# A new order for the beginning of an attention, gated-MLP and soft-MoE kernel: first scores, turned probabilities, and weight blocks in pairs

## The chip, the cores and the metric

The kernel runs on one core of one Trainium2 chip. The metric is the device time of one execution in microseconds (us). Three executions of the kernel before took 1693.24, 1691.48 and 1683.35 us, median 1691.48 us.

## The reference

Three stages follow each other, all in float32:

```python
# attention, 8 batches x 12 heads, 448 positions, head size 64
q_n, k_n = rmsnorm(q, g_q), rmsnorm(k, g_k)
attn = softmax(q_n @ k_n.T / 8)          # rows sum to 1 (+1e-9)
x = (attn @ v) as (3584 tokens, 768)
# gated MLP, 768 -> 1536 -> 768
x = (sigmoid(x @ w_gate) * (x @ w_val)) @ w_out
# soft MoE: 32 slots, 8 experts of 4 slots, 768 -> 1024 -> 768
logits = x @ phi
d = softmax(logits over tokens); c = softmax(logits over slots)
out = c @ expert_mlps(d.T @ x)
```

## The kernel before

**Tiling.** The heads are taken in 48 pairs, six pairs to a batch. For one pair (`slot`) the kernel loads q, k and v, normalises q and k (`prep_a` to `prep_g`), and makes seven score tiles of up to 128 rows by 448. The gated MLP of a batch (the "products", `mm`, line 805) starts when all six pairs of that batch are done. It has 72 units over the twelve weight blocks of `w_gate` and `w_val` and 36 units over `w_out`. The soft MoE follows the MLP batch by batch, and the experts come at the end.

**One score tile in the first twelve pairs** (batches 0 and 1, done in float32) goes through five steps. `score`: TensorE makes the tile `sc` (L434, L428 for the tail). `soft_max`: VectorE scales it and takes the row maximum (L470). `soft_exp`: ScalarE makes `p` or `ps` with row sums (L490). `soft_hi`: TensorE turns the probabilities in four transposes (`pq`, L499). `soft_lo`: ScalarE copies the turned tile out of PSUM into a buffer (L532). When all tiles of a pair are there, `weigh` makes the row sums (`rs`, L576 and L582) and the product with v (`av`, L590) on TensorE, and three small operations (L609 to L612) put the result into `ck`, from which the MLP reads. From pair 12 on the attention runs in float16 along another path, which the change does not touch.

**Weights.** The float32 weights go through a conversion into two float16 halves before the MLP of batch 0 can use them. A gate/value block has two tiles (gate and value, 128 x 768 each). One tile costs a load into one of two `wr` buffers (L712), three VectorE operations that move bits (`to_f32`: L694, L697, L700) into a scratch region `x` of the still unused `gt` buffer (a ring of `NX` regions), and one ScalarE pass that finds a size (`amax`, L677). For a block, two small TensorE products spread the sizes over the partitions (`am`, L129), five or six small VectorE operations make scales (`w_scale`), and then each tile takes two ScalarE scalings (L742, L743) and one GpSimd subtraction (L744). `w_out` has twelve more tiles with the same bit moves and `amax`, two scalings (L772, L773), one subtraction (L774) and a store to a DRAM scratch `wos`, from which the MLP's second half loads `wo`.

**What sets the order.** All work is entered in an agenda, a table of numbered steps: `at(g, fn)` puts a function at step g. A head pair takes 18 steps (`G0` holds the starts), the MLP of batch 0 starts at step `M0` = 115, and each batch of it takes 108 steps with six products in a step. The list `LEN` sets the steps of pairs 6 to 11. The constants at the top (`KN`) place the conversions: before, blocks 0 to 5 sit at steps 18, 33, 48, 63, 78 and 93, blocks 6 to 11 at 111, 114, ... 126, and the `w_out` tiles every fourth step from 117. Up to step 259 the agenda gives only a first order: the tile layer (`schedule_with_timeline_sim=True` on the launch line) reorders each engine's queue within the dependences by a timeline that it computes. From step 259 on the order of the agenda holds as it is (`manual_schedule`).

Within an engine instructions run in the order of its queue. TensorE's scores, transposes, `am` products and MLP products share one queue. VectorE's row maxima share one with the bit moves, ScalarE's exponentials with `amax`, the scalings, the copies and the MLP's sigmoid. In the trace each change between exponentials (L490) and sigmoids (L811) shows an ACT_TABLE_LOAD.

Of the kernel before, what the change touches and what calls it, by code (L numbers as in the profile page):

```python
# [23 lines left out]
def kernel(  # L24
# [26 lines left out]
    NP = H // 2  # L51
# [87 lines left out]
    pe_t = wte[:, 3072 * 7:3072 * 12]  # L139
# [89 lines left out]
    def v_first():  # L229
        x = gt.rearrange("p f a s -> p (f a s)").bitcast(F32)[:, 0:6 * S]  # L230
        sp.dma_start(out=x, in_=v[0].rearrange("h s d -> (h s d)").rearrange("(p e) -> p e", p=128))
        t = smp.tile([128, 8], F32, tag="vam", name="vam")
        vec.tensor_reduce(out=t[:, 6:7], in_=x, axis=AX.X, op=ALU.max, apply_absolute_value=True)
        vec.tensor_scalar(out=t[:, 6:7], in0=t[:, 6:7], scalar1=1e-30, scalar2=None, op0=ALU.max)
# [381 lines left out]
    def slot(j):  # L616
# [7 lines left out]
        for i, o in enumerate((0, 0, 5, 5, 10, 10, 14) if j < JP else (0, 2, 5, 7, 10, 13, 15)):  # L624
# [5 lines left out]
                (3, lambda i=i: soft_hi(j, i)),  # L630
                (4, lambda i=i: soft_lo(j, i)),
# [811 lines left out]
```

## Time and profile before

| | |
|---|---|
| the profiled execution's own time | 1691.47 us |
| its span in the trace | 1689.7 us |
| instructions | 26467 |
| TensorE busy | 1562.3 us (92%) |
| VectorE busy | 1055.4 us (62%) |
| ScalarE busy | 936.6 us (55%) |
| GpSimd busy | 634.7 us (38%) |
| first score product starts | 30.12 us |
| first MLP product starts (end of "stage 1" below) | 168.17 us |
| last product with v of pair 11 ends (end of "stage 2") | 413.3 us |

A row of a timeline gives the start, the busy time, the engine, the line, the operation, what it writes and reads, the shape and the count, and in brackets how long its engine had been idle and who ended that. A row of a windows view gives for a stretch the busy time and number of instructions of each engine, then the TensorE clock that was granted (1.00 is full), the share of DMA time and GB/s. A row of a groups view gives busy time and the mean in ns of one, then the idle time of the engine just before the group's instructions and what ended it. On TensorE each float32 product appears as two records.

### The profile page before, as it was taken

The numbers are of one execution on the slowest core, as the hardware profiler recorded it, in microseconds if no ns is written. First come the engines' busy times: TensorE is split into PE (matmuls) and PEld (weight loads), VectorE is DVE, ScalarE is ACT, GpSimd is POOL, SyncE is SP. The second block draws the span as 40 slices with busy tenths as digits, with TensorE's granted clock in tenths as the row PEclk, the third lists the DMA queues.
The fourth block names the chain that finished last, engine by engine and source line by source line (L and its number), as shares of the span: only waits on it lengthen the run. The fifth ranks groups of instructions, "written<-read, shape, count | busy, mean of one in ns | idle before, by whom it ended". The sixth has DMA issues, their size and how long they took to land.

```text
span 1689.7 us, 26467 instructions
## 1 busy us (share of the span) xinstructions
PE 1562.3 (92%) x9065; PEld 777.8 (46%) x9065; DVE 1055.4 (62%) x2602; ACT 936.6 (55%) x1795; POOL 634.7 (38%) x725
## 2 busy tenths in 40 slices
PE   3887678999999999999999999999999999999985
PEld 1444334454454454545444545454545454555323
DVE  6677876545667777767776777677767663310214
ACT  3777668744766566656655665466656663211113
POOL 3445533336234535454545454535454530000000
PEclk9898789999999999999999999999999999999876
DMA  6344455325448755774688468756884566444899
GB/s 204 91 132 147 148 164 161 103 71 127 92 109 175 178 106 138 179 185 95 148 163 189 92 153 164 159 108 138 180 183 96 129 141 191 149 153 150 315 376 328
DMA packets 508021, 266.55 MB, mean 158 GB/s; under 512 B 403568, under 2 KB 476016, under 8 KB 507760
## 3 DMA queue, kind: packets, MB, share of 16 engines
q1 hardware_dynamic: 500976, 227.13, 53.6%
q10 hardware_dynamic: 6912, 37.75, 7.2%
q8 instruction: 71, 1.16, 0.3%
q14 instruction: 62, 0.51, 0.1%
HBM read 162.96 MB, written 15.73 MB: 106 GB/s over the span
## 4 chain that ended last, share of the span: by engine, by line
PE 48%; DVE 8%; ACT 8%; DMA 5%; issue 3%; SPq 2%; POOL 0%; ACTq 0%; POOLq 0%; DVEq 0%
PE mm L805 32%; DMA uni<-pst 4%; PE av L597 4%; PE sc L451 3%; DVE pst L548 2%; ACT pst L509 2%; PE so L961 2%; PE hp L1180 1%; PE tx L948 1%; ACT p L490 1%; DVE sc L470 1%; PE po L1232 1%; ACT sgf L811 1%; DVE ss L272 1%; ACT L490 1%
## 5 line engine op out<-in xcount | busy, mean ns | idle before, releaser
L805 PE MATMUL mm<-ck,wt 128*128 128x448 f16 x3456 | 706.1, 354 | 0.9 <-DVE ck L612 0.9
L805 PEld LDWEIGHTS <-wt 128*128 128x128 f16 x3456 | 330.7, 98 | 323.9 <-issue 40.2
L805 PE MATMUL mm<-gt,wo 128*128 128x448 f16 x1728 | 347.5, 353 | 2.5 <-DMA wo<-wos 2.4
L509 ACT ACTIVATE pst<-p,sm 128x448 f16<-128x448 f32 x252 | 168.2, 668 | 222.5 <-DVE sm L505 133.6
L548 DVE SCALAR_TENSOR_TENSOR pst<-p,sm,pst 128x448 f16<-128x448 f32 x252 | 204.6, 812 | 96.3 <-ACT pst L509 87.5
L511 POOL COPY pst<-pst 128x64 f16<-128x64 f16 x252 | 63.9, 254 | 516.7 <-ACT pst L509 516.7
L490 ACT ACTIVATE p<-sc,sm 128x448 f32<-128x448 f32 x286 | 179.6, 628 | 126.5 <-DVE sc L470 123.5
L805 PEld LDWEIGHTS <-wo 128*128 128x128 f16 x1728 | 166.4, 98 | 165.0 <-issue 12.6
L470 DVE TENSOR_SCALAR_CACHE_REDUCE sc<-sc,scal 128x448 f32<-128x448 f32 x252 | 171.5, 681 | 15.8 <-PE sc L451 9.3
L305 POOL TENSOR_TENSOR rr<-ss,nhalf 128x16 f32<-128x16 f32 x48 | 149.1, 3107 | 48.2 <-DVE ss L275 27.6
L451 PE MATMUL sc<-qkt 128*128 128x448 f16 x432 | 116.9, 353 | 0.2 <-DMA qkt<-uni 0.2
L502 DVE TENSOR_SCALAR sm<-sm 128x1 f32<-128x1 f32 x252 | 37.3, 148 | 100.8 <-ACT p L490 100.3
L597 PE MATMUL av<-uni 128*64 128x448 f16 (+1 forms) x792 | 89.8, 361 | 6.7 <-DMA uni<-pst 6.7
L821 DVE TENSOR_TENSOR gt<-sgf,gt 128x448 f16<-128x448 f32 x96 | 76.3, 795 | 11.2 <-ACT gt L820 11.1
L820 ACT CAST gt<-sgf 128x448 f16<-128x448 f32 x96 | 53.5, 557 | 52.4 <-DVE sgf L816 48.6
L816 DVE SCALAR_TENSOR_TENSOR sgf<-mm,fcomp,sgf 128x448 f32<-128x448 f32 x84 | 56.9, 678 | 38.6 <-PE mm L805 38.3
L811 ACT ACTIVATE sgf<-mm,kgate 128x448 f32<-128x448 f32 x96 | 58.3, 632 | 39.7 <-PE mm L805 39.1
L470 DVE TENSOR_SCALAR_CACHE_REDUCE sc<-sc,ss 128x448 f32<-128x448 f32 x84 | 56.2, 684 | 28.5 <-PE sc L434 24.6
L265 POOL TENSOR_TENSOR qn<-rq 128x512 f32<-128x512 f32 x47 | 59.4, 1264 | 33.6 <-DMA rq<-in_q_dram 28.8
L597 PEld LDWEIGHTS <-uni 128*64 128x64 f16 (+1 forms) x792 | 43.5, 110 | 56.3 <-issue 29.9
L811 ACT ACT_TABLE_LOAD x51 | 65.4, 1283 | 4.3 <-PE mm L805 3.4
L265 POOL TENSOR_TENSOR kn<-rk 128x512 f32<-128x512 f32 x47 | 54.7, 1164 | 30.2 <-PE qt L385 17.5
(230 smaller groups left out, 2092.6 us busy)
## 6 DMA issues: line engine op xcount, KB each, us to landing
wo<-wos ACTq DMA_DIRECT2D x48, 768.0 KB, 4.8
wt<-in_moe_w_dram SPq DMA_DIRECT2D x18, 1024.0 KB, 9.7
x<-in_moe_w_dram SPq DMA_DIRECT2D x12, 1024.0 KB, 10.7
vl<-in_v_dram SPq DMA_DIRECT2D x42, 224.0 KB, 2.7
rq<-in_q_dram SPq DMA_DIRECT2D x48, 192.0 KB, 2.7
rk<-in_k_dram SPq DMA_DIRECT2D x48, 192.0 KB, 2.8
wr<-in_moe_w_gate_dram SPq DMA_DIRECT2D x12, 768.0 KB, 4.4
wr<-in_moe_w_val_dram SPq DMA_DIRECT2D x12, 768.0 KB, 4.4
```

Of the source, the lines that this page charges most:

```text
L265: pool.tensor_tensor(out=x, in0=raw[j][i], in1=raw[j][i], op=ALU.mult)
L305: pool.tensor_tensor(out=rr, in0=ss, in1=nhalf, op=ALU.pow)
L451: pe.matmul(out=ps, lhsT=qk[:, 3 * h, 128 * t + 128:128 * t + 256], rhs=qk[:, 3 * h + 1 + n, TAIL:512], start=(n == 0), stop=(n == 1),)
L470: vec.tensor_scalar(out=ps, in0=ps, scalar1=ne, scalar2=3e38, op0=ALU.mult, op1=ALU.min, accum_out=sm[:, 1:2])
L490: act.activation(out=p, in_=ps, func=AF.Exp, scale=-1.0 if KN.get("ACC", 0) else esc, bias=sm[:, 1:2], accum_out=total)
L509: act.activation(out=st[:, 0:S], in_=p, func=AF.Copy, scale=sm[:, 3:4])
L511: pool.tensor_copy(out=st[:, S:S + TAIL], in_=st[:, 0:TAIL])
L548: ins = vec.scalar_tensor_tensor(out=st[:, S + TAIL:], in0=p, scalar=sm[:, 3:4], in1=st[:, 0:S], op0=ALU.mult, op1=ALU.subtract)
L597: pe.matmul(out=ps[64 * h:64 * h + 64, :], lhsT=vs[0:kk, hl, h, tv, :], rhs=pt[h][0:kk, tp, :], start=(n == 0), stop=(n == len(passes) - 1),)
L805: pe.matmul(out=ps, lhsT=l, rhs=r, start=(n == 0 and m == 0), stop=(n == last and m == len(terms) - 1))
L811: act.activation(out=sgm, in_=mm_t.pop(("g", f)), func=AF.Sigmoid, scale=kgate[:, b % 2, f:f + 1])
L821: later(2, lambda: vec.tensor_tensor(out=gt[:, f, 1, :], in0=gf, in1=gt[:, f, 0, :], op=ALU.subtract))
```

## The change

The change has four parts, three of them by constants.

1. **The beginning.** The gains are loaded from ScalarE's queue before everything else (`gains_load`), together with a dummy exponential that loads the table. The search for the largest v of batch 0 (`v_first_max`, then `am` and its scale) leaves the beginning and stands at steps 4, 6 and 8. The copies that make `sel` move to step M0+20, and `phi` goes straight to its place, with three copies at M0+30 instead of four at the start.
2. **The turn of P.** For pairs 0 to 11 `soft_hi` and `soft_lo` stand six and seven steps behind their scores instead of three and four. The next scores of a pair stand five steps behind.
3. **Weights in twos.** Blocks 2n and 2n+1 share one `am` of four columns and one set of scales. Blocks 0/1 are entered at step 2, then 28, 54, 80, 104 and 122 (`GV`), the second block's tiles six steps later (`GD`), the scalings at 16 and 17 steps (`GW`). So eight of twelve blocks are entered within batch 0's attention instead of six. The scratch ring has six regions instead of four, and the turned P of pairs 0 to 5 goes to the buffer `uni` instead of to the part of `wt` that blocks 7 to 11 will fill.
4. **Room.** Pairs 6 to 11 take 18 steps each instead of 28 and five times 16, and the `w_out` tiles start ten steps later (`WOF` 12 instead of 2).

```diff
-KN=json.loads('{... "WOF": 2, ... "NX": 4, ... "LEN": [28, 16, 16, 16, 16, 16], ...
-  "ORD": "sel qk0 a0 g qk1 w b0 c0 d0 e0 f0 g0 a1 v0 vf v1 phi", ...}')
+KN=json.loads('{... "WOF": 12, ... "NX": 6, ... "LEN": [18, 18, 18, 18, 18, 18], ...
+  "ORD": "gl qk0 sel a0 qk1 w b0 g c0 d0 e0 f0 g0 a1 v0 vf v1 phi", ...
+  "VF": 4, "GV": [2, 28, 54, 80, 104, 122], "GW": 16, "GD": 6}')
-    pe_t = wte[:, 3072 * 7:3072 * 12]
...
+    def v_first_max():
         t = smp.tile([128, 8], F32, tag="vam", name="vam")
-        vec.tensor_reduce(out=t[:, 6:7], in_=x, axis=AX.X, op=ALU.max, apply_absolute_value=True)
+        vec.tensor_reduce(out=t[:, 6:7], in_=vam_t.pop("x"), axis=AX.X, op=ALU.max, apply_absolute_value=True)
         vec.tensor_scalar(out=t[:, 6:7], in0=t[:, 6:7], scalar1=1e-30, scalar2=None, op0=ALU.max)
         vam_t[0] = t
-        vamax_spread(0)
-        vamax_scale(0)
...
-                        pt = (pe_t if j < NP else uni)[:, 3584 * n:3584 * n + 3584]
+                        pt = uni[:, 3584 * n:3584 * n + 3584]
...
-                (3, lambda i=i: soft_hi(j, i)),
-                (4, lambda i=i: soft_lo(j, i)),
+                (3 + 3 * (j < JP), lambda i=i: soft_hi(j, i)),
+                (4 + 3 * (j < JP), lambda i=i: soft_lo(j, i)),
...
+    def w_spread(f):
+        w_t["m", f] = spread_max(w_t["s", f // 2][:, 0:4], 4)
...
+        def gains_load():
+            gl = first["gl"] = p1.tile([128, 2, D], F32, tag="t3", name="gl", bufs=3)
+            for i, g in enumerate((g_q, g_k)):
+                act.dma_start(out=gl[:, i, :], in_=g.unsqueeze(0).to_broadcast([128, D]))
+            act.activation(out=scal[:, 2:3], in_=nhalf1, func=AF.Exp)
...
+        at(KN["VF"], v_first_max)
+        at(KN["VF"] + 2, lambda: vamax_spread(0))
+        at(KN["VF"] + 4, lambda: vamax_scale(0))
+        at(M0 + 20, blocks_of_sel)
+        at(M0 + 30, more_columns)
...
+            for n in range(2):
+                for i in range(2):
+                    if f + n >= EW:
+                        at(g + KN["GD"] * n, lambda n=n, i=i: w_load(f + n, i))
+                    at(g + 2 + KN["GD"] * n + i, lambda n=n, i=i: w_bits(f + n, i))
+            e = g + KN["GW"]
+            at(e - 2, lambda: w_spread(f))
+            at(e - 1, lambda: w_scale(f))
+            at(e - 1, lambda: gate_scales(0, f, f + 2))
+            for n in range(2):
+                at(e + n, lambda n=n: w_split(f + n))
```

What the tile layer makes of it is seen in the engines' queues. Lines of the changed kernel are one lower in the middle of the file and up to twelve higher at its end (L434 is now L433, L805 now L808). Three places follow.

TensorE, the first rows of its queue, before (`gt`, `qt`: gains, q and k turned; `vam`: the largest v):

```order
L1292 MATMUL gt<-ident,gl 128x128
L388 MATMUL qt<-ident,rq 64x128 x8
L385 MATMUL qt<-ident,kn 128x128 x4
L129 MATMUL am<-ident,vam 128x128
L434 MATMUL sc<-qkt 128x448 x4
L499 MATMUL pq<-ident,p 128x128 x4
```

and now:

```order
L1301 MATMUL gt<-ident,gl 128x128
L387 MATMUL qt<-ident,rq 64x128 x8
L384 MATMUL qt<-ident,kn 128x128 x4
L433 MATMUL sc<-qkt 128x448 x4
L498 MATMUL pq<-ident,p 128x128 x8
L498 MATMUL pq<-ident,ps 128x128 x4
L129 MATMUL am<-ident,vam 128x128
```

The `am` product of v stood ahead of the first four scores and stands behind them and three turned tiles.

VectorE, the queue ahead of pair 0's first row maxima, before (`gt<-wr`: bit moves of a weight tile; `ss`: sums of squares):

```order
L233 TENSOR_REDUCE vam<-gt 128x1
L1303 COPY gt<-pl 128x6x32 x4
L234 TENSOR_SCALAR vam<-vam 128x1
L694 TENSOR_SCALAR gt<-wr 128x768
L133 TENSOR_REDUCE vam<-am 128x1
L697 SCALAR_TENSOR_TENSOR gt<-wr,gt 128x768
L121 TENSOR_SCALAR sg<-vam 128x1
L272 TENSOR_REDUCE ss<-qn 128x8
L700 SCALAR_TENSOR_TENSOR gt<-wr,gt 128x768
L225 RECIPROCAL sg<-sg 128x1
L470 TENSOR_SCALAR sc,sm<-sc,ss 128x448 x2
```

and now:

```order
L699 SCALAR_TENSOR_TENSOR gt<-wr,gt 128x768
L693 TENSOR_SCALAR gt<-wr 128x768
L274 TENSOR_SCALAR ss<-ss 128x16
L469 TENSOR_SCALAR sc,sm<-sc,ss 128x448
L696 SCALAR_TENSOR_TENSOR gt<-wr,gt 128x768
...
L234 TENSOR_REDUCE vam<-gt 128x1
L308 TENSOR_SCALAR ss<-rr,scal 128x8
L469 TENSOR_SCALAR sc,sm<-sc,ss 128x448
L1313 COPY gt<-gt 128x6x32 x3
```

Before, three weight tiles and the search in v stood ahead of the first maximum. Now one tile and the start of the next do, and three maxima stand ahead of the search in v. Up to the first maximum of pair 1 there are now five tiles and two thirds of a sixth in the queue, and there were four. The sixteen `sel` copies stand in VectorE's second row before and now.

TensorE early in the MLP of batch 0, before, where single `am` products stand:

```order
L805 MATMUL mm<-ck,wt 128x448
L129 MATMUL am<-ident,wa 128x128
L434 MATMUL sc<-qkt 128x448 x2
L499 MATMUL pq<-ident,p 128x128 x4
L499 MATMUL pq<-ident,ps 128x128 x4
```

and now, at the first `am` behind the MLP's start:

```order
L808 MATMUL mm<-ck,wt 128x448
L129 MATMUL am<-ident,wa 128x128 x4
L433 MATMUL sc<-qkt 128x448 x2
...
L498 MATMUL pq<-ident,ps 128x128 x4
L498 MATMUL pq<-ident,p 128x128 x4
```

Before, single `am` products of fresh tiles stood between products, the scores and their own turned tiles with nothing between (44 products without any score had gone ahead). Now four `am` stand together, nine products stand where "..." is, and the turned tiles behind them belong to earlier scores. Behind the product with v of pair 11 the queues of all engines are the same but for names.

More of the change, by code (lines that the diff above doesn't have):

```diff
@@ L1275 @@
         EW = KN.get("EW", 1)
+        first = {}
+        def gains_load():
[3 more added lines that the diff above has]
+            act.activation(out=scal[:, 2:3], in_=nhalf1, func=AF.Exp)
         def gains():
-            gl = p1.tile([128, 2, D], F32, tag="t3", name="gl", bufs=3)
-            for i, g in enumerate((g_q, g_k)):
-                sp.dma_start(out=gl[:, i, :], in_=g.unsqueeze(0).to_broadcast([128, D]))
+            gl = first["gl"]
             gm = smp.tile([128, 4], F32, tag="wa", name="gm")
@@ L1299, in slots_to_columns, with more_columns @@
         def slots_to_columns():
-            pl = p1.tile([128, KD, NS], F32, tag="t3", name="pl", bufs=3)
-            sp.dma_start(out=pl, in_=phi.rearrange("(c p) s -> p c s", p=128))
-            for m in range(4):
-                vec.tensor_copy(out=phr[:, :, m, :], in_=pl)
+            sp.dma_start(out=phr[:, :, 0, :], in_=phi.rearrange("(c p) s -> p c s", p=128))
+        def more_columns():
+            for m in range(1, 4):
+                vec.tensor_copy(out=phr[:, :, m, :], in_=phr[:, :, 0, :])
         def w_first():
@@ L1316 @@
         ops = dict(
-            sel=make_sel, qk0=lambda: load_qk(0), g=gains, qk1=lambda: load_qk(1), w=w_first,
+            sel=make_sel, gl=gains_load, qk0=lambda: load_qk(0), g=gains, qk1=lambda: load_qk(1), w=w_first,
             a0=lambda: prep_a(0), b0=lambda: prep_b(0), c0=lambda: prep_c(0), d0=lambda: prep_d(0),
@@ L1324 @@
         assert not ops
[L1326 to L1336 removed]
+        at(KN["VF"], v_first_max)
[3 more added lines that the diff above has]
+        at(M0 + 30, more_columns)
+        def gv(g, f):
+            assert g + KN["GW"] <= M0 + 12 * (f // 2), "gv late"
+            for n in range(2):
[9 more added lines that the diff above has]
+                at(e + n, lambda n=n: w_split(f + n))
         def wo(g, f):
@@ L1341, in wo @@
             at(g + KN.get("WB", 2), lambda: wo_split(f))
-        NPRE = KN.get("NPRE",4)
-        for f in range(NPRE):
-            gv(G0[NP] - KN.get("PS",20) * (NPRE - f), f)
-        for f in range(NPRE, KF):
-            gv(M0 + KN.get("GO",0)+KN.get("GS",6) * (f - NPRE), f)
+        for n, g in enumerate(KN["GV"]):
+            gv(g, 2 * n)
         for f in range(KF):
```

40 lines of the change are left out of this document (16 added, 24 removed).

## The prediction

> **What bounds the kernel now.** I read the busy times by stretch first, with the cuts at the first score, the first MLP product, the end of the weight conversions and the end of pair 11's product with v.
>
> ```profile
> core 0: us, PE busy (x) PEld busy (x) DVE busy (x) ACT busy (x) POOL busy (x), PEclk, DMA share, GB/s
> 0.00:30.12 30.12, 4.16 (x23) 2.97 (x23) 17.49 (x49) 5.74 (x10) 12.92 (x16) 1.00 0.77 232
> 30.12:168.16 138.04, 116.39 (x623) 59.16 (x622) 100.47 (x237) 100.95 (x220) 63.53 (x50) 0.89 0.42 124
> 168.16:345.00 176.84, 142.34 (x790) 73.52 (x790) 124.06 (x261) 129.57 (x220) 69.60 (x49) 0.90 0.49 140
> 345.00:413.30 68.30, 67.16 (x406) 34.17 (x405) 31.19 (x75) 31.06 (x70) 28.52 (x27) 1.00 0.36 102
> 413.30:1689.70 1276.40, 1232.23 (x7230) 607.98 (x7228) 782.21 (x1981) 669.26 (x1276) 460.12 (x584) 0.98 0.66 165
> 140.00:160.00 20.00, 14.73 (x84) 7.80 (x82) 19.12 (x34) 13.75 (x30) 11.60 (x7) 0.88 0.54 160
> 240.00:320.00 80.00, 69.37 (x398) 34.56 (x398) 50.72 (x117) 65.60 (x112) 32.64 (x24) 0.98 0.49 127
> ```
>
> From 345 us on TensorE is the bound (67.16 of 68.30, then 1232 of 1276 us). Before that no engine is: in the second and third row VectorE and ScalarE are both busy 70 to 73% of the time, and TensorE waits 22 and 34 us and runs at a clock of 0.89 and 0.90. The order behind 413.3 us is the same in both kernels, so I take these 1276.4 us as unchanged, and the question is when pair 11 ends. What TensorE waits for, first between 30 and 168 us, then between 168 and 413 us:
>
> ```profile
> PE pq L499 <- ACT ps L490: 11.5, 9, 2.7
> PE pq L499 <- ACT p L490: 7.8, 7, 2.2
> ```
>
> ```profile
> PE am L129 <- ACT wt L677: 18.6, 3, 10.8
> PE pq L499 <- ACT p L490: 6.8, 4, 3.7
> PE qt L385 <- ACT uni L532: 3.5, 2, 2.6
> ```
>
> In the first stretch it is the turn of a tile that waits for that tile's exponential. In the second it is `am`, which waits for the size of a weight tile and holds up the whole queue. These are the two waits at which the change is aimed.
>
> **The beginning.** The timeline of TensorE, then single rows of the other engines:
>
> ```profile
> 12.58 0.45 PE L1292 MATMUL gt<-ident,gl 128*128 128x128 f32 x1 [12.58 <-DVE gl L1290]
> 15.86 1.09 PE L385 MATMUL qt<-ident,kn 128*128 128x128 f32 x4 [0.92 <-ACT qkt L396]
> 29.40 0.79 PE L129 MATMUL am<-ident,vam 128*128 128x128 f32 x2 [12.45 <-DVE vam L234]
> ```
>
> ```profile
> 10.77 0.23 DVE L1282 TENSOR_TENSOR ggn<-gl 128x64 f32<-128x64 f32 x1 [3.16 <-DMA gl<-in_g_k_dram]
> 11.16 2.92 POOL L305 TENSOR_TENSOR rr<-ss,nhalf 128x16 f32<-128x16 f32 x1 [9.86 <-DVE ss L275]
> 16.98 0.59 ACT L400 COPY qkt<-qt 128x512 f32<-128x512 f32 x1 [1.25 <-PE qt L385]
> 25.53 2.94 DVE L233 TENSOR_REDUCE vam<-gt 128x1 f32<-128x2688 f32 x1
> 47.44 0.69 DVE L470 TENSOR_SCALAR_CACHE_REDUCE sc<-sc,ss 128x448 f32<-128x448 f32 x1 [0.24 <-PE sc L434]
> ```
>
> Two waits go. VectorE stood 3.16 us for the gains, and the scale of pair 0's rows (L275, then GpSimd's L305) stood behind. With the gains issued first I take about 2.8 us off. Pair 0's q and k are turned at 16.98 + 0.59 = 17.57 us, yet TensorE then idles to 29.40 us for the `am` of v. With `am` behind the scores they start at 17.57 - 2.8, about 15 us, instead of 30.12.
>
> Of these 15 us little reaches the end of pair 0, since VectorE's queue now brings weight tiles there. From the first maximum (about 19 us, behind one tile) to that of pair 1 its rows add up to 22.6 us: seven maxima at 0.61 start to start, 2.94 for v, nearly five tiles at about 2.45, and small ones. Two `wr` buffers, each reloaded behind the last bit move of its tile, add about 2 us. So pair 1 starts at about 44 us, where the row above has 47.44: 3.5 us of time and 1.7 tiles (4 us) of work ahead. The dummy exponential, the fourth `phi` copy and the `sel` copies (which the queue leaves where they were) I set at nothing; together they are under 2 us of engines that wait there anyway.
>
> **Stage 1, to the first MLP product.** The groups of 0 to 168 us, VectorE's and ScalarE's:
>
> ```profile
> L470 DVE TENSOR_SCALAR_CACHE_REDUCE sc<-sc,ss 128x448 f32<-128x448 f32 x45 | 30.3, 682 | 8.5 <-PE sc L434 6.6 <-PE sc L428 1.9
> L697 DVE SCALAR_TENSOR_TENSOR gt<-wr,gt 128x768 int32<-128x768 int32 x16 | 18.6, 1160 | 0.0
> L700 DVE SCALAR_TENSOR_TENSOR gt<-wr,gt 128x768 int32<-128x768 int32 x16 | 15.7, 980 | 0.0
> L694 DVE TENSOR_SCALAR gt<-wr 128x768 int32<-128x768 int32 x16 | 13.3, 831 | 4.7 <-POOL wt L744 4.7
> ```
>
> ```profile
> L677 ACT ACTIVATE wt<-gt 128x768 f16<-128x768 f32 x16 | 13.5, 845 | 16.8 <-DVE gt L700 16.1 <-DVE su L536 0.3
> L743 ACT ACTIVATE gt<-gt,wa 128x768 f32<-128x768 f32 x14 | 12.6, 932 | 0.0
> L742 ACT ACTIVATE wt<-gt,wa 128x768 f16<-128x768 f32 x14 | 12.3, 932 | 2.4 <-DVE wa L735 2.4
> ```
>
> The new queue has 20 tiles' bit moves ahead of the end of stage 1 and 16 tiles' scalings, for 16 and 14. VectorE's work there rises from 118.0 us (17.49 + 100.47) by 4 x (0.83 + 1.16 + 0.98) = 11.9 us and falls by about 3 for the scales made in twos: 127 us. ScalarE's rises from 106.7 by 4 x 1.03 + 4 x 0.93 = 7.8 to 114.5 us. So this stage does more work and gains only if the engines fill. They should: a turn now stands behind the next scores, so TensorE has 0.5 to 4 us of other work while an exponential is made, and the 19.3 us of the first wait view shrink. I bound the filling by the table: 73% as now, 95.6% as in 140 to 160 us (19.12 of 20). From 15 us on VectorE has 127 - 8 = 119 us left. At 73% the stage ends at 178 us, at 95% at 140. I take 85%, the middle: 155 us, 13 us earlier than 168.16.
>
> One thing speaks against more. ScalarE now gets up to eight scalings in a row (8 x 0.93 = 7.5 us) ahead of a `ck` and a copy of turned tiles, and was given four before. While they run TensorE has a product with v and one to three scores, about 4 to 5 us.
>
> The clock could add to the gain. An `am` among products takes 0.38 us, one behind a long wait 0.80:
>
> ```profile
> 182.83 0.38 PE L129 MATMUL am<-ident,wa 128*128 128x128 f32 x2
> 196.17 0.80 PE L129 MATMUL am<-ident,wa 128*128 128x128 f32 x2 [10.84 <-ACT wt L677]
> ```
>
> The Trainium skill ("TensorE: Matmul & The Clock Gate", Part 1) says that the clock falls to half behind about 3.4 us of idleness and comes back behind as much work; these rows agree. By it a TensorE without long waits would need some 14 us less for the 142.34. I leave this out of the sum, as ScalarE and not TensorE sets the pace below.
>
> **Stage 2, to pair 11's product with v.** The single `am` products are gone from TensorE's queue, pairs 6 to 11 are spread evenly, and a tile's turn has a dozen products ahead of it. So the 18.6 us wait should vanish. What is late next is ScalarE. It has 129.57 + 31.06 = 160.6 us here, less the 7.8 us moved to stage 1, so 152.8. Behind the last `w_out` tile of the new queue stand some 28 us of it, so the dense part has 125 us. The rows that are dear in it:
>
> ```profile
> L490 ACT ACT_TABLE_LOAD x10 | 12.8, 1283 | 0.2
> L772 ACT ACTIVATE hl<-x,wa 128x768 f16<-128x768 f32 x12 | 11.2, 930 | 5.9 <-DVE wa L771 5.9
> L677 ACT ACTIVATE hl<-x 128x768 f16<-128x768 f32 x12 | 10.1, 845 | 10.5 <-POOL hl L774 5.0 <-DVE wa L734 3.9 <-DVE x L700 1.7
> ```
>
> At 73% these 125 us take 171, at 90% 139. I take the 82% of 240 to 320 us (65.60 of 80.00), the densest stretch where both kinds of work ran: 152 us. TensorE's own work there is about 118 us at full clock, so it waits for ScalarE. Behind it come 237 products and the attention of two pairs. A product takes (403.84 - 399.30) / 24 = 0.189 us:
>
> ```profile
> 399.30 4.70 PE L805 MATMUL mm<-gt,wo 128*128 128x448 f16 x24
> 403.84 0.60 PE L499 MATMUL pq<-ident,ps 128*128 128x128 f32 x4
> ```
>
> That is 45 us, and about 31 us for the attention, as in the 68.30 us now. Stage 2 takes 152 + 76 = 228 us, for 245.1 before: 17 us less.
>
> A table load costs the dense part 1.28 us each, twenty times:
>
> ```profile
> 201.09 1.28 ACT L490 ACT_TABLE_LOAD   x1
> 202.38 0.63 ACT L490 ACTIVATE p<-sc,sm 128x448 f32<-128x448 f32 x1
> ```
>
> The Trainium skill ("ScalarE: Activation LUTs", What ACT_TABLE_LOAD costs) gives 1283 ns for a load, as here, and 1380 ns more for draining the engine, 2.66 us a switch. By that 20 switches would cost 53 us instead of 26. No run shows the drain: the work ahead ends at 201.08, the exponential starts 1.29 us later. The row decides.
>
> **Sum.** 155 + 228 = 383 us for 413.3, so 30.3 us less. The profiled span becomes 1659.4 us; with the 1.8 us between span (1689.7) and time (1691.47, the median of the runs to 0.01 us) it is 1661 us.
>
> **Rivals.** *The engines fill.* With 93% of VectorE in stage 1 (15 + 128 = 143 us) and 90% of ScalarE in stage 2 (139 + 76 = 215) pair 11 ends at 358: 1636 us. For it: 140 to 160 us shows 95.6%. Against it: both queues are in order, and each waits for the other (16.1 us of `amax` for L700).
>
> *Filling stays at 73%.* 178 + 171 + 76 = 425 us: 1703 us. The beginning is then swallowed by the work moved ahead. For it: VectorE's and ScalarE's shares are the same 70 to 73% in two stages with different orders; the ring of six regions still makes the third tile of each group of four wait for GpSimd's subtraction of the group before. Against it: the 19.3 and 18.6 us of waits by name.
>
> *The runs of eight scalings go uncovered.* Six pairs of blocks, each holding up the copies and `ck`, and so TensorE, by 7.5 us: 45 us against the 8 us won by pair 1, 1728 us; with TensorE's 4 us in between half is covered, 1707. It makes the kernel slower by over 1% from 4.2 us uncovered a run. Against it: the runs of four cost TensorE no named wait.
>
> **How the numbers follow.** I give my sum (1645 to 1674) 62%, the filling engines 17%, unchanged filling (1675 to 1708) 16%, the uncovered runs 5%. So faster by over 1% has 0.79, within 1% 0.16, slower 0.05; 1% is about what a measurement of this kernel tells from no change. The range of 8 in 10 is 1638 to 1686: down to the filled engines, up into unchanged filling.
>
> **What would show it.** Right: the first scores at 14 to 16 us, the first maximum at 18 to 21 and that of pair 1 at 42 to 46; the first MLP product at 148 to 162; no `am` wait over 2 us behind it; ScalarE at 80% or more until the last `w_out` tile; pair 11's end at 370 to 397; 1276 us behind it, within 3. Wrong: a first MLP product behind 168 us, a TensorE wait over 4 us in each run of scalings, or a difference behind 413 us.

## The result, and the profile after

The changed kernel takes 1671.87 us (median of four executions, 1666.34 to 1672.9); before, four executions gave 1687.41 us (1683.26 to 1693.24). The ratio is 0.9891, with a 95% interval of 0.9848 to 0.9933: 11 in a thousand faster. The forecast was 1661 us, in a range of 1638 to 1686: 30.3 us less than before, where the medians differ by 15.5. The profiled execution took 1671.93 us, and its span is 1670.1 us.

The windows view with the new cuts (first score 15.46, first MLP product 176.10, 324 between ScalarE's last pass over a `w_out` tile and GpSimd's, end of pair 11's product with v 397.80):

```profile
core 0: us, PE busy (x) PEld busy (x) DVE busy (x) ACT busy (x) POOL busy (x), PEclk, DMA share, GB/s
0.00:15.46 15.46, 3.44 (x22) 2.48 (x22) 8.16 (x35) 4.18 (x7) 5.84 (x11) 1.00 0.65 192
0.00:176.10 176.10, 127.47 (x649) 67.81 (x650) 136.60 (x281) 112.86 (x243) 87.57 (x68) 0.84 0.51 154
176.10:397.80 221.70, 204.36 (x1194) 106.12 (x1192) 136.95 (x302) 156.90 (x280) 96.47 (x80) 0.98 0.48 132
176.10:324.00 147.90, 130.56 (x757) 68.55 (x755) 98.85 (x217) 120.64 (x204) 61.33 (x44) 0.97 0.47 132
324.00:397.80 73.80, 73.80 (x439) 37.57 (x438) 38.10 (x86) 36.26 (x77) 35.14 (x36) 1.00 0.50 132
397.80:1670.10 1272.30, 1227.88 (x7225) 605.92 (x7225) 779.33 (x1984) 668.93 (x1275) 455.61 (x578) 0.98 0.66 165
```

and of the kernel before, with one row each for its two stages:

```profile
0.00:168.16 168.16, 120.55 (x645) 62.13 (x645) 117.96 (x286) 106.69 (x230) 76.45 (x66) 0.91 0.48 143
168.16:413.30 245.14, 209.50 (x1194) 107.69 (x1194) 155.25 (x335) 160.63 (x290) 98.12 (x76) 0.93 0.45 129
```

Stage 1 became longer, 176.1 us for 168.2. Stage 2 became shorter, 221.7 for 245.1. Pair 11 ends at 397.8 us, 15.5 us earlier.

The last subtraction of a `w_out` tile ends at 315.3 us in the kernel before and at 326.3 in the change. Two rows of before with that cut, then the change's first part:

```profile
168.16:315.32 147.16, 112.66 (x610) 58.43 (x610) 109.90 (x224) 111.51 (x189) 61.92 (x39) 0.88 0.53 149
315.32:413.30 97.98, 96.84 (x587) 49.26 (x585) 45.35 (x111) 49.12 (x102) 36.20 (x37) 1.00 0.34 99
176.10:326.30 150.20, 132.86 (x772) 70.10 (x770) 100.16 (x222) 122.91 (x206) 63.30 (x47) 0.97 0.48 132
```

So the part with conversions did not become shorter, 150.2 us for 147.2. TensorE does more in it, 132.9 us for 112.7 and at a clock of 0.97 for 0.88, and that leaves 71.5 us behind it for 98.0.

TensorE's waits in the changed kernel, from the first score to the first MLP product, then in stage 2:

```profile
PE rs L581 <- ACT ps L489: 7.5, 2, 5.4
PE pq L498 <- ACT p L489: 5.5, 6, 2.2
PE am L129 <- ACT ps L489: 5.0, 1, 5.0
PE pq L498 <- ACT ps L489: 4.7, 5, 1.5
PE qt L384 <- ACT uni L531: 3.9, 2, 3.3
PE pq L498 <- ACT uni L531: 3.0, 2, 2.5
```

```profile
PE mm L808 <- ACT sgf L814: 4.8, 2, 3.2
PE av L589 <- ACT uni L531: 3.8, 1, 3.8
PE pq L498 <- ACT qkt L395: 3.3, 2, 2.4
PE am L129 <- ACT wt L676: 2.5, 1, 2.5
```

Both named waits shrank. That of `pq` for exponentials went from 19.3 to 10.2 us (5.5 + 4.7), that of `am` for weight sizes from 18.6 to 2.5 us. But in stage 1 other rows have taken their place: the row sums (`rs`), `am` and `qt` now wait for ScalarE, 16 us together. TensorE's idle time in the same stretch, 15 to 168 us, is 153.00 less its busy time: 35 us before and 37 us now, at a lower clock. Of before, then of the change:

```profile
15.00:168.00 153.00, 118.03 (x628) 60.37 (x628) 112.48 (x256) 103.94 (x226) 71.90 (x59) 0.90 0.48 143
```

```profile
15.00:168.00 153.00, 116.21 (x588) 61.24 (x588) 125.80 (x240) 105.31 (x226) 79.06 (x55) 0.84 0.51 153
```

The timeline of the beginning, TensorE's rows and then VectorE's:

```profile
15.46 3.35 PE L433 MATMUL sc<-qkt 64*128 64x448 f32 x8 [0.68 <-ACT qkt L399]
...
26.41 0.80 PE L129 MATMUL am<-ident,vam 128*128 128x128 f32 x2 [2.08 <-DVE vam L235]
```

```profile
18.56 0.68 DVE L469 TENSOR_SCALAR_CACHE_REDUCE sc<-sc,ss 128x448 f32<-128x448 f32 x1
...
40.76 0.68 DVE L469 TENSOR_SCALAR_CACHE_REDUCE sc<-sc,ss 128x448 f32<-128x448 f32 x1
```

The first scores start at 15.46 us for 30.12, and the `am` of v stands behind four of them. The last row is the first maximum of pair 1, the eighth of all: 40.76 us for 47.44.

VectorE's bit moves to the end of stage 1 (groups of 0 to 176.1 us):

```profile
L696 DVE SCALAR_TENSOR_TENSOR gt<-wr,gt 128x768 int32<-128x768 int32 x20 | 25.9, 1294 | 0.2
L699 DVE SCALAR_TENSOR_TENSOR gt<-wr,gt 128x768 int32<-128x768 int32 x20 | 25.3, 1265 | 0.1
L693 DVE TENSOR_SCALAR gt<-wr 128x768 int32<-128x768 int32 x20 | 17.5, 874 | 5.3 <-POOL wt L747 4.1 <-DMA wr<-in_moe_w_val_dram 1.1
```

There are 20 tiles, as counted, but a tile takes 3.43 us where it took 2.97. GpSimd's and VectorE's rows of one stretch show where the time goes (L747: the subtraction of a weight tile; L264: the squares of q's rows):

```profile
79.26 7.47 POOL L747 TENSOR_TENSOR wt<-gt,wt 128x768 f16<-128x768 f32 x4 [8.39 <-ACT gt L746]
86.69 1.35 POOL L264 TENSOR_TENSOR qn<-rq 128x512 f32<-128x512 f32 x1
80.93 1.98 DVE L693 TENSOR_SCALAR gt<-wr 128x768 int32<-128x768 int32 x1 [3.07 <-POOL wt L747]
82.95 2.28 DVE L696 SCALAR_TENSOR_TENSOR gt<-wr,gt 128x768 int32<-128x768 int32 x1
85.15 0.68 DVE L469 TENSOR_SCALAR_CACHE_REDUCE sc<-sc,ss 128x448 f32<-128x448 f32 x1
...
87.07 1.79 DVE L699 SCALAR_TENSOR_TENSOR gt<-wr,gt 128x768 int32<-128x768 int32 x1
88.78 0.94 DVE L696 SCALAR_TENSOR_TENSOR gt<-wr,gt 128x768 int32<-128x768 int32 x1
...
93.82 0.54 DVE L693 TENSOR_SCALAR gt<-wr 128x768 int32<-128x768 int32 x1
```

While the four subtractions of a pair of blocks run on GpSimd (79.26 to 86.73 us), a move takes 1.98 and 2.28 us. When GpSimd is done the same moves take 0.54 and 0.94. It is not the subtraction alone: behind the four a move takes 1.79 us beside GpSimd's L264, where the shortest of its line takes 0.94. A row maximum beside the subtractions, which reads PSUM, keeps its 0.68.

### The profile page after: what moved, and what is told of

Same layout as the page of the kernel before. It is cut to its first block, busy times and chain, and to the rows that moved or that the text cites. A ratio compares the mean times of both kernels' runs of the same rounds, so it can differ in the third digit from the quotient of the medians.

```text
span 1670.1 us, 26410 instructions
## 1 busy us (share of the span) xinstructions
PE 1559.7 (93%) x9065; PEld 779.9 (47%) x9065; DVE 1052.9 (63%) x2565; ACT 938.7 (56%) x1798; POOL 639.6 (38%) x725
## 4 chain that ended last, share of the span: by engine, by line
PE 48%; ACT 7%; DVE 6%; DMA 5%; issue 3%; SPq 2%; POOL 1%; ACTq 0%; POOLq 0%; DVEq 0%
PE mm L808 34%; PE av L596 4%; DMA uni<-pst 4%; PE sc L450 3%; DVE pst L547 2%; PE so L964 1%; PE hp L1183 1%; ACT pst L508 1%; PE tx L951 1%; ACT sgf L814 1%; ACT p L489 1%; PE po L1235 1%; ACT L489 1%; ACT L814 1%; DVE sc L469 1%
## 5 line engine op out<-in xcount | busy, mean ns | idle before, releaser
L808 PE MATMUL mm<-ck,wt 128*128 128x448 f16 x3456 | 703.7, 353 | 4.9 <-ACT sgf L814 4.8
L808 PEld LDWEIGHTS <-wt 128*128 128x128 f16 x3456 | 330.2, 98 | 325.3 <-issue 40.2
L808 PE MATMUL mm<-gt,wo 128*128 128x448 f16 x1728 | 348.0, 353 | 0.6 <-DMA wo<-wos 0.4
L508 ACT ACTIVATE pst<-p,sm 128x448 f16<-128x448 f32 x252 | 168.2, 667 | 218.0 <-DVE sm L504 138.9
L547 DVE SCALAR_TENSOR_TENSOR pst<-p,sm,pst 128x448 f16<-128x448 f32 x252 | 200.9, 797 | 92.8 <-ACT pst L508 83.1
L808 PEld LDWEIGHTS <-wo 128*128 128x128 f16 x1728 | 166.2, 98 | 163.0 <-issue 12.4
L264 POOL TENSOR_TENSOR qn<-rq 128x512 f32<-128x512 f32 x47 | 59.8, 1273 | 39.0 <-DMA rq<-in_q_dram 39.0
L264 POOL TENSOR_TENSOR kn<-rk 128x512 f32<-128x512 f32 x47 | 55.9, 1189 | 19.2 <-PE qt L384 6.2
```

Of the source, the lines that this page charges most:

```text
L264: pool.tensor_tensor(out=x, in0=raw[j][i], in1=raw[j][i], op=ALU.mult)
L508: act.activation(out=st[:, 0:S], in_=p, func=AF.Copy, scale=sm[:, 3:4])
L547: ins = vec.scalar_tensor_tensor(out=st[:, S + TAIL:], in0=p, scalar=sm[:, 3:4], in1=st[:, 0:S], op0=ALU.mult, op1=ALU.subtract)
L808: pe.matmul(out=ps, lhsT=l, rhs=r, start=(n == 0 and m == 0), stop=(n == last and m == len(terms) - 1))
```

## The experiments

The theory ahead of them: part 3, the weights in twos, took away in stage 1 what parts 1 and 2 won there. The rivals: the beginning or the later turn did not bring what the forecast says, or the runs of scalings cost it.

Twelve kernels ran in three groups of four, in the order of the table, each group beside the kernel before. "Pair 5" and "pair 11" are the ends of these pairs' products with v in the profiled execution. Pair 5's is taken as the end of stage 1 from here on, since in some orders the first MLP products run ahead of it; for the kernel before it is 166.7 us, for the change 175.9 (the expectation of twos_late has 175.5, the end of the last product but one). "Behind" is the span less pair 11.

| kernel | first MLP product | pair 5 | pair 11 | behind | median us (range) | ratio to before (95%) |
|---|---|---|---|---|---|---|
| before | 168.2 | 166.7 | 413.3 | 1276.4 | 1689.6 (1683.1 to 1696.5) | |
| the change | 176.1 | 175.9 | 397.8 | 1272.3 | 1671.9 (1666.3 to 1672.9) | 0.9891 (0.9848 to 0.9933) |
| begin_back | 184.0 | 189.5 | 410.3 | 1274.2 | 1686.9 (1680.9 to 1690.1) | 0.9975 (0.9957 to 0.9993) |
| turn_back | 180.4 | 180.4 | 404.3 | 1276.2 | 1682.0 (1678.2 to 1692.5) | 0.9962 (0.9940 to 0.9985) |
| weights_back | 144.1 | 148.7 | 396.4 | 1275.7 | 1666.6 (1661.1 to 1674.0) | 0.9867 (0.9828 to 0.9905) |
| room_back | 181.4 | 179.9 | 406.2 | 1272.8 | 1674.9 (1672.3 to 1680.7) | 0.9918 (0.9885 to 0.9950) |
| begin_only | 153.4 | 151.0 | 398.1 | 1269.5 | 1673.3 (1669.4 to 1675.8) | 0.9915 (0.9886 to 0.9944) |
| sub_dve | 173.0 | 172.6 | 390.8 | 1273.3 | 1665.2 (1661.3 to 1666.5) | 0.9856 (0.9834 to 0.9877) |
| split_apart | 176.6 | 176.4 | 397.8 | 1272.8 | 1671.8 (1666.1 to 1674.8) | 0.9895 (0.9868 to 0.9921) |
| singles_eight | 164.1 | 168.8 | 390.6 | 1270.6 | 1662.0 (1659.4 to 1667.1) | 0.9844 (0.9819 to 0.9870) |
| twos_late | 160.8 | 167.1 | 398.3 | 1272.1 | 1672.9 (1670.7 to 1677.4) | 0.9904 (0.9879 to 0.9928) |
| eight_sub | 157.2 | 166.8 | 391.6 | 1271.8 | 1663.7 (1660.6 to 1665.4) | 0.9837 (0.9816 to 0.9859) |
| eight_sub_all | 153.6 | 162.9 | 387.0 | 1274.8 | 1662.3 (1660.0 to 1663.6) | 0.9830 (0.9810 to 0.9850) |
| singles_ten | 167.5 | 175.4 | 392.4 | 1273.1 | 1668.6 (1664.1 to 1670.8) | 0.9867 (0.9846 to 0.9887) |

The row of before has the 19 executions beside the first group; beside the two others its median was 1689.0 and 1690.4, and beside the change it was 1687.4. A fourth execution of begin_only took 3144.33 us; it has no trace, and why is open. It is left out of that row.

Two things limit what a row shows. Ahead of step 259 the tile layer lays the queues anew after each edit, so a run shows an edit together with the order that follows from it. And the columns from the first product to "behind" are of one execution. In eight_sub and eight_sub_all all engines run the same operations in the same order up to pair 5, yet it ends at 166.8 and at 162.9 us. So a difference of 4 us in these columns shows nothing by itself. The profiled executions of room_back and weights_back are moreover the slowest of their four, 5.8 and 7.3 us over the median.

**begin_back: part 1 undone.**

```diff
-  "ORD": "gl qk0 sel a0 qk1 w b0 g c0 ..."
+  "ORD": "sel qk0 a0 gl g qk1 w b0 c0 ..."
-                act.dma_start(out=gl[:, i, :], in_=g.unsqueeze(0).to_broadcast([128, D]))
-            act.activation(out=scal[:, 2:3], in_=nhalf1, func=AF.Exp)
+                sp.dma_start(out=gl[:, i, :], in_=g.unsqueeze(0).to_broadcast([128, D]))
...
-vf=v_first
+vf=lambda: (v_first(), v_first_max(), vamax_spread(0), vamax_scale(0))
-        at(KN["VF"], v_first_max)
...
```

> The changed kernel with part 1 undone alone: gains loaded from SyncE's queue without the dummy exponential, sel and phi copies and the search in v of batch 0 at the start, as before. Theory (the 6.7 us that the first row maximum of pair 1 comes earlier, 40.76 for 47.44 us, reach the end of pair 11): first scores at about 30 us, pair 1's first maximum at 46 to 48, the first MLP product at about 182 for 176.1, pair 11's end at about 404 for 397.8, some 1678 us. Rival (they are swallowed, because weight tiles set VectorE's pace from there on): first MLP product and pair 11's end within 2 us of the changed kernel, 1670 to 1674 us.

Measured: first scores at 30.67 us, pair 1's first maximum at 52.81, pair 11 at 410.3, 12.5 us later than with part 1, and 15.0 us more in the medians. The rival falls, and the old beginning costs most of the whole gain. The theory's direction holds, but all its figures behind the first scores are too small: pair 1's maximum is 12 us later and not 6.7, since with part 3 two weight tiles more stand ahead of it than in the kernel before (18 moves and not 12). What holds of the mechanism is that the shift goes through: 12 us at pair 1, 12.5 at pair 11.

**turn_back: part 2 undone.**

```diff
-                (3 + 3 * (j < JP), lambda i=i: soft_hi(j, i)),
-                (4 + 3 * (j < JP), lambda i=i: soft_lo(j, i)),
+                (3, lambda i=i: soft_hi(j, i)),
+                (4, lambda i=i: soft_lo(j, i)),
```

> The changed kernel with part 2 undone alone: the turn of P three and four steps behind its scores again. Theory (the turn behind the next scores is what took TensorE's waits for exponentials from 19.3 to about 10 us ahead of the first MLP product): these waits are back at 18 us or more, the first MLP product comes 5 to 10 us later, at 181 to 186, and pair 11's end at 403 to 410; 1677 to 1684 us. Rival (VectorE's pace decides there, a wait that goes in one place comes back in another): first MLP product within 3 us of 176.1, time within 3 us of the changed kernel.

Measured: 180.4 us, pair 11 at 404.3, 10.1 us more in the medians. TensorE's waits for exponentials from 15 to 181 us:

```profile
PE pq L498 <- ACT ps L489: 20.7, 9, 4.4
PE pq L498 <- ACT p L489: 4.9, 4, 2.3
```

25.6 us, for 10.2 with the later turn. The theory holds in all its parts but the first MLP product, which lies 0.6 us under its bracket. Of the 15.4 us of waits that the later turn saves, 4.5 are left at pair 5's end in these profiles and 6.5 at pair 11's. Most of the rest of the 10.1 lies behind pair 11 (1276.2 us for 1272.3), where nothing was changed.

**weights_back: part 3 undone.** The functions `w_bits` to `w_split`, `gv` and its loops of the kernel before, with its constants (six of twelve blocks in batch 0, ring of four, turned tiles of pairs 0 to 5 in `wt`), the other three parts kept.

> The changed kernel with part 3 undone alone: single blocks at the old steps, six of twelve in batch 0, a ring of four scratch regions. Theory (the work moved ahead and its bit moves beside GpSimd's subtractions cost stage 1 what the other parts won): the first MLP product at 152 to 162 us for 176.1, VectorE's 16 tiles at about 2.95 us a tile for 3.43; in stage 2 the waits of am for a weight size are back with 10 us or more and it takes 235 to 250 us for 221.7, so pair 11's end at 392 to 405 and 1666 to 1680 us. Rival (twos are what gains in both stages): first MLP product at 170 or later and pair 11's end at 410 or later, over 1684 us. Second rival (the twos lose on the whole): pair 11's end at 390 or earlier, under 1664 us.

Measured: 144.1 us to the first MLP product, better than the theory's bracket, and 252.3 us from there to pair 11, over its 250 (247.7 from pair 5 to pair 11). TensorE's wait for weight sizes is back in stage 2:

```profile
PE am L129 <- ACT wt L677: 18.6, 5, 9.8
```

Pair 11 ends at 396.4 us and the median is 5.2 us lower than the change's. The two intervals overlap, so no loss by part 3 is shown on the whole, but a gain by it isn't either. By these profiles it made stage 1 27.2 us longer and stage 2 25.8 us shorter.

**room_back: part 4 undone.**

```diff
-  "WOF": 12, ... "LEN": [18, 18, 18, 18, 18, 18]
+  "WOF": 2, ... "LEN": [28, 16, 16, 16, 16, 16]
```

> The changed kernel with part 4 undone alone: pairs 6 to 11 at 28 and five times 16 steps, the w_out tiles ten steps earlier. Theory (the even spread only shifts work inside stage 2, whose am waits went with the twos): first MLP product within 2 us of 176.1, no am wait over 3 us behind it, pair 11's end within 3 us of 397.8, 1669 to 1675 us. Rival (the room is what took the 18.6 us of am waits): these waits are back with 8 us or more, pair 11's end at 406 or later, over 1679 us.

Measured: 1674.9 us, in the theory's bracket, and there is no wait of `am` for a weight size in stage 2. But pair 11 ends 8.4 us later and the first MLP product 5.3, which the theory did not have; 406.2 us lies in the rival's bracket. The rival's reason falls with the wait. The medians differ by 3.1 us only, and the profiled execution is the slowest of its four, so a worth of the room is not shown; what it would come from is open.

**begin_only: part 1 alone on the kernel before** (part 1's lines of the diff).

> The kernel before with part 1 of the change alone. Theory (the beginning is worth in this order what it was worth in the changed kernel, 15 us when undone there): first scores at 15.3, the first maximum of pair 1 at 36 to 42 for 47.44, first MLP product at 153 to 160 for 168.2, pair 11's end at 397 to 403 for 413.3, 1672 to 1679 us. Rival (without the later turn TensorE's waits for exponentials swallow it): first MLP product at 163 or later, 1682 us or more.

Measured: pair 1's first maximum at 35.78 us, 11.7 us earlier than in the kernel before, the first MLP product at 153.4, pair 11 at 398.1, 15.2 us earlier. The median is 15.7 us under the 1689.0 of the executions of before beside it. The theory holds (pair 1's maximum 0.2 us under its bracket). Alone, part 1 gives nearly what all four parts give together (0.9915 and 0.9891, with overlapping intervals). The wait for weight sizes stays in stage 2:

```profile
PE am L129 <- ACT wt L677: 18.1, 3, 11.1
```

**sub_dve: the subtraction on VectorE.**

```diff
-            pool.tensor_tensor(out=wt[:, f, :, i, 1, :], in0=x, in1=wt[:, f, :, i, 0, :], op=ALU.subtract)
+            vec.tensor_tensor(out=wt[:, f, :, i, 1, :], in0=x, in1=wt[:, f, :, i, 0, :], op=ALU.subtract)
```

> The changed kernel with the 24 subtractions of gate/value tiles on VectorE in place of GpSimd, nothing else. Theory (bit moves beside a GpSimd subtraction take twice as long, and that is why a tile's three moves cost 3.43 us in the changed kernel's stage 1 for 2.97 before): the three forms go to about 0.56, 0.95 and 0.95 us, 2.5 us a tile, 19 us less for 20 tiles; 16 subtractions of 0.8 to 1.0 us come onto VectorE, 13 to 16 us; the wait of the moves for GpSimd (4.1 us) goes; first MLP product 3 to 10 us earlier than 176.1. Rival (the moves are slow for another reason, such as loads landing in the same buffers): the means stay above 1.1 us for the two longer forms and the first MLP product comes 8 us or more later.

The groups of 0 to 176.1 us:

```profile
L696 DVE SCALAR_TENSOR_TENSOR gt<-wr,gt 128x768 int32<-128x768 int32 x20 | 20.7, 1034 | 0.1
L699 DVE SCALAR_TENSOR_TENSOR gt<-wr,gt 128x768 int32<-128x768 int32 x20 | 19.7, 986 | 0.1
L747 DVE TENSOR_TENSOR wt<-gt,wt 128x768 f16<-128x768 f32 x16 | 16.0, 1003 | 1.9 <-ACT gt L746 1.8
L693 DVE TENSOR_SCALAR gt<-wr 128x768 int32<-128x768 int32 x20 | 14.5, 725 | 5.2 <-DMA wr<-in_moe_w_val_dram 3.6 <-DMA wr<-in_moe_w_gate_dram 1.5
```

The moves fall from 3.43 to 2.75 us a tile. Three moves with GpSimd idle take 0.55 + 0.95 + 0.95 = 2.45 us, so about two thirds of what a tile cost above that came from the subtractions. The longest that are left, up to 1.80 us, run beside GpSimd's operations on q and k rows (L264, L312). VectorE's sum, though, is no smaller: 54.9 us of moves and 16.0 of subtractions, for 68.7. Still the first MLP product comes 3.1 us earlier, as the theory has it, and pair 11 7.0 us earlier, 6.7 us in the medians. The intervals overlap (up to 0.9877, and from 0.9848), so the gain is likely and not shown. That GpSimd's queue no longer waits for ScalarE (8.39 us ahead of 79.26 us in the fence above) may be the reason; no run takes that apart.

**split_apart: shorter runs of scalings.**

```diff
-                at(e + n, lambda n=n: w_split(f + n))
+                at(e + (6 if f < 8 else 1) * n, lambda n=n: w_split(f + n))
```

> The changed kernel with the scalings of the second block of the first four pairs of blocks six steps later, so that at most four of them follow each other by the agenda. Theory (the runs of up to eight scalings are not what costs stage 1; VectorE's slowed moves and its waits are): first MLP product within 4 us of 176.1, time within 4 us of the changed kernel. Rival (the runs hold up copies and ck, 4 us a run): 8 to 16 us earlier, first MLP product at 160 to 168 us and 1656 to 1664 us.

Measured: 176.6 us, pair 11 at 397.8, 1671.8 us. But the edit did not reach the engines: the tile layer set the same order again. In the traces of this kernel and of the change every engine runs the same operations in the same order (9065 on TensorE, 2565 on VectorE, 1798 on ScalarE, 725 on GpSimd), with seven scalings on end from 47.6 us here and 47.3 there. So the run says nothing on shorter runs of scalings. It is the changed kernel a second time, and its median is the same to 0.1 us.

What the runs of scalings cost is seen in the change's own trace. A window over the first run of seven, then ScalarE's and TensorE's rows about a run of four:

```profile
47.30:53.20 5.90, 5.90 (x30) 2.15 (x26) 1.97 (x4) 5.90 (x9) 1.54 (x1) 1.00 0.42 123
```

```profile
112.59 3.41 ACT L745 ACTIVATE wt<-gt,wa 128x768 f16<-128x768 f32 x4 [3.26 <-DVE wa L738]
115.91 0.61 ACT L489 ACTIVATE ps<-sc,sm 128x448 f32<-128x448 f32 x1
116.67 1.55 PE L581 MATMUL rs<-ident,su 128*64 128x128 f32 x12 [5.39 <-ACT ps L489]
```

Beside this long run TensorE is busy all the time, and beside the runs of six and seven from 74.9 and 149.4 us for 5.02 of 5.10 and 5.90 of 5.90 us. At 112.59 us an exponential stands behind four scalings whose scales came late from VectorE, and TensorE waits 5.39 us for it. So in these places it is not the length of a run that holds up TensorE, but its place ahead of an exponential. What another place would bring no run here shows.

**singles_eight: eight single blocks.**

```diff
-  "NPRE": 6, "PS": 15
+  "NPRE": 8, "PS": 12
-                        pt = (pe_t if j < NP else uni)[:, 3584 * n:3584 * n + 3584]
+                        pt = uni[:, 3584 * n:3584 * n + 3584]
```

(against weights_back)

> The kernel without part 3, but eight of twelve blocks in batch 0: single blocks twelve steps apart from step 12 on, turned tiles of pairs 0 to 5 in the buffer of the changed kernel, ring of four regions. It tells the twos from the eight blocks. Theory (it is the twos, late sizes and scalings in a heap beside GpSimd, that took the 32 us in stage 1, more than the 12 us of ScalarE and 12 us of VectorE that four tiles bring): first MLP product at 152 to 160 us for 144.1 with six single blocks, stage 2 at 228 to 238 us, pair 11's end at 384 to 394 for 396.4, 1653 to 1664 us. Rival (it is the moved work): first MLP product at 168 or later, pair 11's end 396 or later, 1666 us or more.

Measured: pair 11 at 390.6 us and 1662.0 us, in the theory's brackets; the first MLP product at 164.1 lies between the two. The windows of weights_back, cut at pair 5 and pair 11:

```profile
0.00:148.70 148.70, 118.31 (x652) 62.02 (x653) 113.97 (x286) 104.92 (x230) 72.65 (x64) 0.92 0.53 160
148.70:396.41 247.71, 215.94 (x1192) 110.67 (x1191) 155.35 (x332) 162.36 (x291) 104.27 (x84) 0.92 0.47 132
```

and of singles_eight, with its longest `am` wait for a weight size behind 144 us:

```profile
0.00:168.78 168.78, 130.97 (x658) 68.43 (x659) 136.06 (x310) 115.48 (x246) 82.94 (x69) 0.82 0.52 156
168.78:390.56 221.78, 206.56 (x1184) 106.34 (x1185) 141.72 (x308) 151.74 (x276) 96.45 (x80) 0.97 0.48 136
```

```profile
PE am L129 <- ACT wt L676: 1.9, 1, 1.9
```

Two blocks more in batch 0 cost stage 1 20.1 us and save stage 2 25.9 us. With single blocks, too, the `am` wait goes and stage 2's clock rises to 0.97. So eight blocks ahead of the MLP are enough to end this wait, without the twos. The difference of 4.6 us in the medians is not shown (the intervals overlap). Against eight single blocks the twos lose 7.1 us by pair 5, 7.2 by pair 11 and 9.9 in the medians. Why is not taken apart: the twos are entered earlier, and up to seven scalings follow each other where it is at most four here.

**twos_late: the same twos, entered later.**

```diff
-  "GV": [2, 28, 54, 80, 104, 122]
+  "GV": [12, 34, 57, 80, 104, 122]
```

> The changed kernel with only the first three entries of its table of pairs of blocks later: 12, 34 and 57 steps for 2, 28 and 54. Theory (the twos lose to the eight single blocks in one place, the start, where the fifth and sixth weight tile stand on VectorE between the last maximum of pair 0 and the first of pair 1: pair 0's product with v ends at 50.1 us for 42.5, pair 5's at 175.5 for 168.8): pair 0's ends at 42 to 45, pair 5's at 167 to 171, pair 11's at 388 to 393, 1661 to 1666 us. Rival (the heap of four late scalings and GpSimd beside VectorE cost it again later): pair 5's at 174 or later, 1669 us or more.

Measured: pair 5 ends at 167.1 us, 8.8 us earlier, in the theory's bracket, though pair 0 does not (50.8). But pair 11 ends at 398.3 us: the 8.8 us are given back in stage 2. The rival's time came, not its place, so this theory falls. Part of it is work that was put off: by pair 5's end 56 moves are done for 60, and VectorE has 129.0 us of work there for 136.5 and 143.4 for 137.0 in stage 2. Why the rest is lost again is open.

**eight_sub and eight_sub_all: singles_eight with subtractions on VectorE,** first those of the gate/value tiles (as in sub_dve), then the `w_out` tiles' as well.

```diff
-        pool.tensor_tensor(out=hl[:, 1, :], in0=x, in1=hl[:, 0, :], op=ALU.subtract)
+        vec.tensor_tensor(out=hl[:, 1, :], in0=x, in1=hl[:, 0, :], op=ALU.subtract)
```

> The kernel with eight single blocks in batch 0 and the subtractions of gate/value tiles on VectorE. Theory (what VectorE's moves lose beside GpSimd is 7 us by pair 11's end in the changed kernel, and single blocks lose about as much, 2.95 us a tile here): pair 11's end at 382 to 387 for 390.6, 1653 to 1658 us. Rival (with single blocks the subtraction is short and apart, so VectorE only gets more work): pair 11's end at 389 to 396, 1661 to 1668 us.

> The same with the twelve subtractions of w_out tiles on VectorE too. Theory (in stage 2 ScalarE and not VectorE sets the pace, and VectorE's moves of w_out tiles stop being slowed): pair 11's end 1 to 4 us earlier than with the gate/value tiles alone. Rival (VectorE's queue there holds up maxima and the MLP's sums): 3 us or more later.

Measured: pair 11 at 391.6 and 387.0 us for 390.6, 1663.7 and 1662.3 us for 1662.0. With single blocks the rival of the first holds: VectorE's busy time up to pair 11 is 277.4 us for 277.8, so the subtractions cost what the moves save. Of the second the profile shows 4.6 us, a little more than its theory has, but 3.9 of them by pair 5, where both kernels run the same order and no `w_out` subtraction. In stage 2, where the theory puts its gain, it is 0.7 us, and in the medians 1.4. No gain is shown.

**singles_ten: ten single blocks.**

```diff
-  "NPRE": 8, "PS": 12
+  "NPRE": 10, "PS": 10
```

> Eight single blocks made ten in batch 0, ten steps apart from step 8. Theory (a block moved ahead costs stage 1 about what it saves in stage 2; six to eight cost 20 us and saved 26): pair 5's product with v ends 16 to 24 us later than 168.8, stage 2 is shorter by as much within 6 us, 1657 to 1668 us. Rival (TensorE is full in stage 2 by then, so that nothing more is saved): pair 11's end 10 us or more later than 390.6, 1672 us or more.

Measured: pair 5 6.6 us later, stage 2 4.8 us shorter (217.0), pair 11 at 392.4, 1668.6 us, 0.6 over the theory's range and short of the rival's. A block moved still costs about what it saves, but the one was set three and the other four times too high.

## Why the prediction was right or wrong

The direction and the range were right, and the time lies 11 us over the forecast. That it isn't more is luck: stage 1 took 21.1 us more than forecast, stage 2 6.3 and the rest 4.1 less. The first MLP product behind 168 us, which I had named as a sign of being wrong, came. Point by point:

- *The beginning.* First scores (15.46) and first maximum (18.56) lie in their brackets, pair 1's maximum (40.76) 1.2 us ahead of its own. The worth was set too low: 3.5 us of time and 4 us of work ahead, against 12.5 us at pair 11 when undone and 15.2 alone. Between the two maxima stand 13 moves of weight tiles, of which 5 come with part 3 (there are 8 in begin_only); alone, part 1 brings pair 1 to 35.78 us. I had charged the beginning with another part's work.
- *Stage 1: the step that failed.* Two terms, 155 us forecast and 176.1 measured. The work was 136.6 us of VectorE and not 127: I priced four more tiles at 2.97 us each (11.9), and the moves rose by 68.7 - 47.6 = 21.1 us. The price of before already held moves that were slowed beside GpSimd; in the new order it rose to 3.43, and with the subtractions off GpSimd it is 2.75. ScalarE's work was sized well, 112.9 us for 114.5. The filling from 15.46 us on was (136.60 - 8.16) / 160.64 = 80% and not the 85% that I took as the middle. At 85% the measured work would have ended at 166.6 us, so the work is 11.6 us of the miss and the filling 9.5. The moves' size is shown by sub_dve; why the engines filled no better stays open. VectorE's longest waits are those for the product with v (11.0 us, and 10.3 before) and for GpSimd's subtraction (4.1, and 4.7 before).
- *The turn.* Its wait shrank as said, and turn_back takes 10.1 us more, 6.5 of them by pair 11. But TensorE's idle time in stage 1 stayed (35 and 37 us): other waits for ScalarE came in.
- *Stage 2.* 221.7 us for 228. The part up to the last `w_out` tile took 147.9 us at 120.64 / 147.90 = 82% of ScalarE (152 at 82%), the rest 73.8 (76). My cut of before at 345 us as the end of the conversions was wrong: the last `w_out` subtraction ends at 315.3 us, and up to there ScalarE's filling is 111.51 / 147.16 = 76% and not 73%. The `am` wait went to 2.5 us (I had said under 2), but for another reason than I gave: I named the `am` products in fours, the even pairs and the late turns. weights_back keeps the last two and has the wait, 18.6 us; singles_eight has none of the fours and is nearly rid of it. It differs from weights_back in having eight blocks ahead of the MLP for six, and that is what ends the wait.
- *Behind pair 11.* 1272.3 us for 1276.4, outside the 3 us that I allowed. In the fourteen profiles this stretch takes 1269.5 to 1276.4 us without any sign of the change, so I put the 4.1 us down to the scatter of single executions.
- *The rivals.* The engines did not fill (397.8 us, not 358), and filling did not stay at 73%: it was 80% and 82%. That unchanged filling gave 178 us for stage 1, close to the 176.1, is chance, with too little work and too little filling. The long runs of scalings did not hold up TensorE while they ran; one run of four did, by 5.39 us. What came true is near the second in one thing: the beginning's gain was partly used up by the work moved ahead.
- *The sum.* From the medians of undoing: part 1 is worth 15.0 us, part 2 10.1, part 4 3.1 (not told from nothing by its interval), part 3 -5.2 (nor this). They add up to 23 us, for 15.5 to 17.8 measured, so they need not be independent; but medians beside different executions of before scatter by some 3 us.

The clock, which I left out, went both ways. In stage 2 it rose from 0.93 to 0.98, and TensorE's busy time fell by 5.1 us (209.50 to 204.36). In stage 1 it fell from 0.91 to 0.84, and the busy time rose by 6.9 us (120.55 to 127.47).

The best times are those of eight single blocks, 1662.0 us, and of the same with all subtractions on VectorE, 1662.3 us (0.983 of before). They lie some 10 us under the change. The change's order as measured in split_apart, in the same group as singles_eight, has an interval from 0.9868; theirs end at 0.9870 and 0.9850. So the first overlaps it by a hair, and the second lies under it.

## What to carry to other kernels

Work that is moved to another stage has the price of its new neighbours, not that of the row it had: look at who runs beside it there. A long wait that goes with a change may hang on another part of it than the one that aims at it; undo the parts one by one before you credit one. Where several in-order engines are each 70 to 80% busy, a wait that is cut inside the stage comes back in part as waits elsewhere (of 15.4 us 4.5 were left at its end, by two profiles), while a start that was 12 us earlier came through whole. Look in the trace whether an edit of the agenda reached the queues before you read its time as an answer.

## What the runs showed of the hardware

VectorE's integer moves between SBUF buffers slow down beside a GpSimd operation: from 0.54 to 1.98 us and from 0.94 to 2.28 us beside subtractions, to 1.79 us beside L264 in the rows above. With the subtractions on VectorE a tile's moves took 2.75 us for 3.43. The longest move of all (2.40 us) is 1.46 us longer than the shortest of its line, less than the 1.65 us that most subtractions take. The Trainium skill ("SBUF — State Buffer", SBUF: two separate sides) says that the two engines share a pair of ports as a lock held for a whole instruction, which a VectorE operation with two SBUF inputs or in a two-port mode needs. By that rule a move waits for at most the rest of one GpSimd operation, and a maximum that reads PSUM for none; the rows agree with both.
